# Decode attention with a mixer MLP on one core: five buffers of 32 KB per partition become three of 64 KB, and the softmax sums become running ones

## The chip, the cores and the metric

The kernel runs on one core of a Trainium2 chip. The metric is the device time of one execution in microseconds; the median of three runs before the change is 406.61 us (406.59 to 406.79). A core has a matrix engine (PE, with its weight loads shown as PEld), a vector engine (DVE), a scalar engine (ACT), GpSimd (POOL) and SyncE (SP), which here only issues transfers. Sixteen DMA engines carry the transfers of all queues. Data comes from HBM into SBUF (128 partitions); PE writes to PSUM.

## The reference

One token (`S = 1`, `D = 1024`) attends over a cache of 65,536 keys with 32 query heads in 4 groups of 8 that share a K and V, and the same token goes through a small mixer MLP. The result is their sum with the token.

```
xn = _layernorm(x)
# A: attention, Hq=32, Hkv=4, Sk=65536, Dh=128
q = (xn @ wq) per head
scores = einsum("bhqd,bhkd->bhqk", q, k) * (Dh ** -0.5)
p = softmax(scores)
a = einsum("bhqk,bhkd->bhqd", p, v) @ wo
# B: mixer MLP
h  = gelu(layernorm(xn) @ w1)
hs = (h, its four quarters shifted along the sequence) @ w2
x1 = xn + hs
b  = x1 + gelu(layernorm(x1) @ w3) @ w4
out = x + a + b
```

With a sequence of length 1 all four shifted quarters are zero. K and V are 16 MB each for a group (134 MB together), the weights some 36 MB; everything is bf16 and is read once: 169.88 MB.

## The kernel before

The cache of a group is cut into `NT = 4` blocks of `KEYS = 16384` keys; a block of K or V is 4 MB, 32 KB in each of the 128 partitions. All inputs but x pass through a pool `big` of `SLOTS = 5` buffers ("homes") of that size. `items` lists them in order: wq in two parts, then for each group K and V of the blocks 0 to 3 in turn and wo of the group, with w3 (two parts) after block 1 of group 0 and w1 after block 1 of group 1; at the end w2 and w4 in five pieces of 16, 8, 2, 1 and 1 rows of 1024 for each partition. `ensure` (L129) issues each load from SP (L118), four items ahead of the one that is computed; a load waits on SP until its home's last reader is done.

For a block of K (`compute_K`, L342) DVE transposes the home in place in four steps (L353), PE forms the scores from each quarter with the spread-out queries `qst` (L357, 32 matmuls into the PSUM tile `sc`), DVE takes the largest (L361), a short chain between PE and DVE spreads it over the partitions (L363 to L372), ACT takes the exponential (L374, with the row sum) and DVE transposes the result to `pT` (L377). `qst` has two buffers, filled for later groups by GpSimd (L257, L380).

For a block of V (`compute_V`, L382) PE sums `pT` against V into the one PSUM buffer `oacc` (L389, 32 matmuls). Each block has its own maximum. For blocks 0 to 2 ACT copies `oacc` to a tile `ob` (L394). After the last block `group_end` (L399) weighs the four partial results by the exponentials of their maxima (L404 to L414), folds them over the partitions with four matmuls against `selbig` (L417) and one against `sel8big` (L419) and makes `oT5`, with which `compute_wo` adds to the output row in `psB` (L160). w2 and w4 add to the same row; after the last piece of w4, ACT and DVE copy a half of it each and ACT and SP issue a store each (L336 to L340).

At the start x comes in two small loads on ACT's queue (L123, L125). The layernorms, masks and selectors are built from it while wq loads; gelu rows of w3 and w1 are turned round through DRAM on GpSimd's queue (`bounce`, L286).

The order of the instructions in an engine's queue is not the order of the text: the tile framework makes it when it builds the kernel, along with the waits.

Of the kernel before, what the change touches and what calls it, by code (L numbers as in the profile page):

```python
# [15 lines left out]
SLOTS = 5  # L16
KEYS = 16384
LOOKAHEAD = 4
# [4 lines left out]
def kernel(  # L23
# [36 lines left out]
    small = ctx.enter_context(tc.tile_pool(name="small", bufs=2))  # L60
    big = ctx.enter_context(tc.tile_pool(name="big", bufs=SLOTS))
    ppool = ctx.enter_context(tc.tile_pool(name="pp", bufs=2))
    obpool = ctx.enter_context(tc.tile_pool(name="obp", bufs=NT))
    scr_pool = ctx.enter_context(tc.tile_pool(name="scr", bufs=2))
    ogpool = ctx.enter_context(tc.tile_pool(name="ogp", bufs=1))
# [7 lines left out]
    wq_v = A_wq.rearrange("(p c) n -> p c n", c=DC)  # L73
    w3_v = B_w3.rearrange("(p c) f -> p c f", c=DC)
# [5 lines left out]
    w4_start = [sum(W4_PIECES[:i]) for i in range(len(W4_PIECES))]  # L80

    items = [("wq", 0), ("wq", 1)]
    for g in range(HKV):
        for r in range(NT):
            items += [("K", g, r), ("V", g, r)]
            if (g, r) == (0, 1):
                items += [("w3", 0), ("w3", 1)]
            if (g, r) == (1, 1):
                items += [("w1",)]
        items += [("wo", g)]  # L90
    items += [("w2",)] + [("w4", q) for q in range(len(W4_PIECES))]

    st = {}

    def slot():
        return big.tile([P, KEYS], BF16, name="slot")

    def issue(item):
        kind = item[0]
        t = slot()  # L100
        if kind == "wq":
            src = wq_v[:, 4 * item[1]:4 * item[1] + 4, :].rearrange("p c n -> p (c n)")
        elif kind == "w3":
            src = w3_v[:, 4 * item[1]:4 * item[1] + 4, :].rearrange("p c n -> p (c n)")
        elif kind == "w4":
            c0 = w4_start[item[1]]
            src = w4_v[:, c0:c0 + W4_PIECES[item[1]], :].rearrange("p c n -> p (c n)")
        elif kind == "w1":
            src = w1_v
        elif kind == "w2":  # L110
            src = w2_v
        elif kind == "wo":
            src = wo_v[item[1]]
        else:
            cache = A_k_cache if kind == "K" else A_v_cache
            _, g, r = item
            src = cache[0, g, r * KEYS:(r + 1) * KEYS, :].rearrange("(p k) d -> p (k d)", p=P)
        nc.sync.dma_start(out=t[:, 0:src.shape[-1]], in_=src)  # L118
        st[item] = t
# [4 lines left out]
    x_row_bf = const.tile([1, D], BF16, name="x_row_bf")  # L124
# [4 lines left out]
    def ensure(upto):  # L129
        while n_issued[0] <= min(upto, len(items) - 1):  # L130
            issue(items[n_issued[0]])
            n_issued[0] += 1
# [3 lines left out]
    ident_bf = const.tile([P, P], BF16, name="ident_bf")  # L136
    make_identity(nc, ident_bf[:])
# [4 lines left out]
    ones_f = const.tile([P, P], F32, name="ones_f")  # L142
    nc.gpsimd.memset(ones_f[:], 1.0)
    xpad = const.tile([P, DC, 32], BF16, name="xpad")
    nc.gpsimd.memset(xpad[:], 0.0)
    xpad2 = const.tile([P, DC, 32], BF16, name="xpad2")
    nc.gpsimd.memset(xpad2[:], 0.0)
    QW = 4 * 520
    qst = []
    for i in range(2):  # L150
        q_ = const.tile([P, QW], BF16, name=f"qst{i}")
        nc.gpsimd.memset(q_[:], 0.0)
        qst.append(q_)
# [11 lines left out]
    xT = const.tile([P, DC], F32, name="xT")  # L165
    nc.vector.tensor_copy(out=xT[:], in_=x_bf[:])

    def layernorm(src, tag):
        rowsum = const.tile([P, 1], F32, name=f"ln_rowsum_{tag}")
        nc.vector.reduce_sum(out=rowsum[:], in_=src[:], axis=AX.X)  # L170
        pm = ps_M.tile([P, 512], F32, name="pm_ln", tag="pm")
        nc.tensor.matmul(pm[:, 0:1], lhsT=ones_f[:], rhs=rowsum[:], start=True, stop=True)  # L172
        negmean = const.tile([P, 1], F32, name=f"ln_negmean_{tag}")
        nc.vector.tensor_scalar(out=negmean[:], in0=pm[:, 0:1], scalar1=-1.0 / D, scalar2=None, op0=ALU.mult)
        cen = const.tile([P, DC], F32, name=f"ln_cen_{tag}")
        nc.vector.tensor_scalar(out=cen[:], in0=src[:], scalar1=negmean[:, 0:1], scalar2=None, op0=ALU.add)
        sq = const.tile([P, DC], F32, name=f"ln_sq_{tag}")
        rowsq = const.tile([P, 1], F32, name=f"ln_rowsq_{tag}")
        nc.vector.tensor_tensor_reduce(out=sq[:], in0=cen[:], in1=cen[:], scale=1.0, scalar=0.0,
                                       op0=ALU.mult, op1=ALU.add, accum_out=rowsq[:])  # L180
        nc.tensor.matmul(pm[:, 1:2], lhsT=ones_f[:], rhs=rowsq[:], start=True, stop=True)
        std = const.tile([P, 1], F32, name=f"ln_std_{tag}")
        nc.scalar.activation(out=std[:], in_=pm[:, 1:2], func=ACTF.Sqrt, bias=eps_t[:, 0:1], scale=1.0 / D)
        rstd = const.tile([P, 1], F32, name=f"ln_rstd_{tag}")
        nc.vector.reciprocal(out=rstd[:], in_=std[:])
        normed = const.tile([P, DC], F32, name=f"ln_out_{tag}")
# [9 lines left out]
    ln_s1 = const.tile([P, 1], F32, name="ln_s1")  # L196
    nc.vector.tensor_scalar(out=ln_s1[:], in0=rstd1[:], scalar1=1.0, scalar2=None, op0=ALU.add)
    ln_s2 = const.tile([P, 1], F32, name="ln_s2")
    nc.vector.tensor_tensor(out=ln_s2[:], in0=negmean1[:], in1=rstd1[:], op=ALU.mult)
    accx = scr_pool.tile([1, NOUT], F32, name="accx", tag="scr")  # L200
    nc.vector.tensor_scalar(out=accx[:], in0=x_row_bf[:], scalar1=ln_s1[0:1, 0:1], scalar2=ln_s2[0:1, 0:1],
                            op0=ALU.mult, op1=ALU.add)
    for j in range(2):
        row_acc(j, ones_f[0:1, 0:1], accx[0:1, 512 * j:512 * (j + 1)])


    sel32 = const.tile([P, 32], F32, name="sel32")
# [9 lines left out]
    selbig = const.tile([P, 4, P], F32, name="selbig")  # L217
    for cg in range(4):
        nc.vector.tensor_copy(out=selbig[:, cg, :].rearrange("p (hl dd) -> p hl dd", dd=16),
                              in_=sel32[:, 8 * cg:8 * cg + 8].unsqueeze(2).to_broadcast([P, 8, 16]))  # L220
# [4 lines left out]
    psel = const.tile([P, 4, P], BF16, name="psel")  # L225
    iv = ident_bf[:].rearrange("p (b i r) -> p b r i", b=2, r=2)
# [25 lines left out]
    def fill_qst(g, eng):  # L252
        wv = qst[g % 2][:].rearrange("p (cg x) -> p cg x", x=520)[:, :, 0:512].rearrange(
            "p cg (bp c) -> p cg bp c", c=128)
        for a in range(4):
            sl = slice(32 * a, 32 * a + 32)
            eng.tensor_copy(out=wv[sl, :, :, 32 * a:32 * a + 8],  # L257
                            in_=qsel[sl, :, 8 * g:8 * g + 8].unsqueeze(1).to_broadcast([32, 4, 4, 8]))

    def compute_wq(part):  # L260
        wt = st.pop(("wq", part))[:].rearrange("p (c n) -> p c n", n=HQ * DH)
        acc = rows_product("psq", part, wt, xpad, 512, 8)
        if part == 1:
            qrow = scr_pool.tile([P, 2, 512], BF16, name="qrow", tag="scr")
            nc.vector.tensor_copy(out=qrow[:, 0, :], in_=acc[:, 0, :])
            nc.scalar.copy(out=qrow[:, 1, :], in_=acc[:, 1, :])
            del st["psq"]
            pt = ps_M.tile([P, 8, P], BF16, name="pm_qt", tag="pm")
            for bk in range(2):
                for c4 in range(4):  # L270
                    nc.tensor.transpose(pt[:, 4 * bk + c4, :], qrow[:, bk, 128 * c4:128 * c4 + 128], ident_bf[:])

            qT = const.tile([P, HQ], BF16, name="qT")
            for bk in range(2):
                nc.vector.tensor_copy(
                    out=qT[:, 16 * bk:16 * bk + 16].rearrange("p (j c) -> p j c", j=4),
                    in_=pt[:, 4 * bk:4 * bk + 4, :].rearrange("p c (j u) -> p j c u", j=4)[:, :, :, 0])
            pq = ps_M.tile([P, 4, HQ], F32, name="pm_qs", tag="pm")
            for bp in range(4):
                nc.tensor.matmul(pq[:, bp, :], lhsT=psel[:, bp, :], rhs=qT[:], start=(bp == 0), stop=(bp == 3),  # L280
                                 skip_group_check=True)
            nc.vector.tensor_copy(out=qsel[:], in_=pq[:])
            fill_qst(0, nc.vector)
            fill_qst(1, nc.gpsimd)
# [8 lines left out]
    def compute_w3(part):  # L293
        wt = st.pop(("w3", part))[:, 0:4 * F].rearrange("p (c n) -> p c n", n=F)
        acc = rows_product("psh", part, wt, xpad2, FW, 8)
        if part == 1:
            hrow = scr_pool.tile([P, 2, FW], BF16, name="hrow", tag="scr")
            nc.scalar.activation(out=hrow[:], in_=acc[:, :, 0:FW], func=ACTF.Gelu_apprx_tanh)
            del st["psh"]
            st["hT"] = bounce(hrow[:].rearrange("(j u) b n -> j u b n", u=32)[:, 0],  # L300
                              lambda f: f.rearrange("(b j n) -> j b n", b=2, j=4), FC, "h")

    def compute_w1():
        wt = st.pop(("w1",))[:, 0:DC * D].rearrange("p (c n) -> p c n", n=D)
        acc = rows_product("psh1", 0, wt, xpad2, 512, 2)
        h1row = scr_pool.tile([64, 512], BF16, name="h1row", tag="scr")
        nc.scalar.activation(out=h1row[:], in_=acc[0:64, 0, :], func=ACTF.Gelu_apprx_tanh)
        grow = scr_pool.tile([64, 512], BF16, name="grow", tag="scr")
        nc.vector.memset(grow[:], 0.0)
        cq = D // 4  # L310
        for grp, shift in enumerate((1, -1, 2, -2)):
# [161 lines left out]
```

## Time and profile before

| what | value |
|---|---|
| median of three runs | 406.61 us |
| the profiled execution, its own time | 406.69 us |
| its span, first to last instruction | 404.8 us |
| PE / DVE / ACT / POOL busy | 61% / 53% / 9% / 3% |
| read from HBM | 169.88 MB, 420 GB/s over the span |
| L353, transposes of K | x64, 142.3 us, 2281 ns each |
| L357, scores | x512, 131.6 us |
| L389, weighted sum of V | x512, 56.0 us |
| L374, exponential | x16, 17.8 us |
| L409, joining of partial results | x12, 0.75 us each |
| L394, copies of oacc | x12, 586 ns each |

The page divides the span into 40 slices of 10.1 us and gives each engine's busy share in tenths. Groups of instructions are listed by line, with the idle time of the engine before them and what ended it. DVE's longest waits are for K's loads (61.1 us before L353), PE's are for DVE (48.0 us before L389, for `pT`; 40.9 before L357, for the transposes). The granted clock of PE is 0.796 on the mean. The chain of work that ended last is 54% DMA, 23% PE and 17% DVE.

### The profile page before, as it was taken

To read this page: it belongs to the slowest core of one execution; us is meant where nothing else is said; L and a number is where in the kernel's file an instruction comes from. 1 tells how busy PE (TensorE), PEld (TensorE's weight loads), DVE (VectorE), ACT (ScalarE), POOL (GpSimd) and SP (SyncE) were. 2 spreads that over 40 slices of the span, in tenths; PEclk is the share of its full clock that TensorE was granted. 3 is DMA by queue.
4 is the path that set the end of the run, shared out by engine and by line. 5 is a ranking of instruction groups with operands and counts; after the bars stand their busy time and mean duration, and the time that the engine had idled before them with its cause. 6 is when DMAs were issued, how large, how long until landed. Compare 5 with 4: busy or idle time off the path is not lost.

```text
span 404.8 us, 3326 instructions
## 1 busy us (share of the span) xinstructions
PE 245.7 (61%) x1400; PEld 95.7 (24%) x1400; DVE 215.7 (53%) x235; ACT 37.7 (9%) x60; POOL 11.2 (3%) x30
## 2 busy tenths in 40 slices
PE   0385565328475847557657948384659474758456
PEld 0132222103132312112223313131233121213122
DVE  0419474017484848346665847475748383838500
ACT  0101101100201010120210010101010101010100
POOL 5001000000000000000010000000000000000000
PEclk9998878857795778768595868888958797679898
DMA  8999999999999999999999999999999999999993
GB/s 363 415 424 449 418 426 434 430 418 444 434 408 439 447 416 419 458 418 416 447 431 413 437 444 414 435 440 418 430 440 424 428 439 427 425 437 413 440 415 134
DMA packets 7065, 170.11 MB, mean 420 GB/s; under 512 B 1023, under 2 KB 1033, under 8 KB 1418
## 3 DMA queue, kind: packets, MB, share of 16 engines
q1 hardware_dynamic: 6772, 169.87, 98.0%
q8 instruction: 11, 0.18, 0.2%
q0 software_dynamic: 128, 0.02, 0.0%
q10 hardware_dynamic: 150, 0.01, 0.0%
q14 instruction: 4, 0.03, 0.0%
HBM read 169.88 MB, written 0.01 MB: 420 GB/s over the span
## 4 chain that ended last, share of the span: by engine, by line
DMA 54%; PE 23%; DVE 17%; ACT 2%; another core or an unknown queue 1%; issue 1%; DVEq 0%; ACTq 0%
DMA slot<-in_A_k_cache_dram 44%; DVE slot L353 11%; PE sc L357 10%; DMA slot<-in_B_w_dram 7%; PE psB L160 5%; PE oacc L389 4%; DMA x_bf<-in_A_x_dram 3%; DVE pT L377 2%; DVE mx L361 2%; ACT p_sb L374 2%; PE rows L244 1%; PE pm_e L417 1%; DVE m L365 0%; PE pm_mx L363 0%
## 5 line engine op out<-in xcount | busy, mean ns | idle before, releaser
L353 DVE STREAM_TRANSPOSE slot<-slot 128x2048 f32<-128x2048 f32 x64 | 142.3, 2281 | 61.1 <-DMA slot<-in_A_k_cache_dram 61.1
L357 PE MATMUL sc<-slot,qst 128*128 128x512 bf16 x512 | 131.6, 411 | 40.9 <-DVE slot L353 40.9
L389 PE MATMUL oacc<-slot,pT 128*32 128x512 bf16 x512 | 56.0, 616 | 48.0 <-DVE pT L377 48.0
L357 PEld LDWEIGHTS <-qst 128*128 128x128 bf16 x512 | 51.6, 103 | 125.1 <-issue 45.9
L361 DVE TENSOR_REDUCE mx<-sc 128x1 f32<-128x1024 f32 x16 | 19.6, 1225 | 34.7 <-PE sc L357 34.7
L374 ACT ACTIVATE p_sb<-sc,nball 128x1024 bf16<-128x1024 f32 x16 | 17.8, 1114 | 209.8 <-DVE nball L372 209.8
L389 PEld LDWEIGHTS <-pT 128*32 128x32 bf16 x512 | 17.5, 139 | 75.0 <-DVE pT L377 49.4
L377 DVE STREAM_TRANSPOSE pT<-p_sb 128x1024 bf16<-128x1024 bf16 x16 | 19.9, 1245 | 23.3 <-ACT p_sb L374 23.3
L244 PE MATMUL rows<-slot,xpad 128*32 128x512 bf16 (+1 forms) x144 | 13.6, 509 | 6.1 <-DMA slot<-in_B_w_dram 6.1
L363 PE MATMUL pm_mx<-ident_f,mx 128*1 128x128 f32 x16 | 4.3, 270 | 21.1 <-DVE mx L361 21.1
L160 PE MATMUL psB<-slot,oT 128*1 128x512 bf16 x64 | 12.6, 564 | 4.3 <-DVE oT L428 4.3
L394 ACT COPY ob<-oacc 128x512 f32<-128x512 f32 x12 | 7.0, 586 | 58.6 <-PE oacc L389 58.6
L160 PE MATMUL psB<-slot,dst_h 128*1 128x512 bf16 x56 | 7.9, 444 | 3.2 <-DMA slot<-in_B_w_dram 3.2
L370 PE MATMUL pm_mx<-ident_f,rep 1*128 1x1 f32 x16 | 3.5, 222 | 9.9 <-DVE rep L367 9.9
L417 PE MATMUL pm_e<-og,selbig 128*128 128x128 f32 x32 | 7.4, 403 | 3.4 <-DVE og L409 3.4
L244 PEld LDWEIGHTS <-xpad 128*32 128x32 bf16 x144 | 5.7, 127 | 15.0 <-issue 13.7
L172 PE MATMUL pm_ln<-ln_rowsum_a,ones_f 128*128 128x1 f32 x2 | 0.6, 348 | 13.6 <-DVE psel L229 13.6
L337 DVE CAST out<-psB 64x256 bf16<-64x256 f32 x1 | 0.4, 417 | 15.2 <-ACT out L336 15.2
L363 PEld LDWEIGHTS pm_mx<-ident_f,mx 128*1 128x1 f32 x16 | 1.3, 79 | 29.0 <-DVE mx L361 29.0
L417 PEld LDWEIGHTS pm_e<-og,selbig 128*128 128x128 f32 x32 | 6.3, 293 | 6.7 <-DVE og L409 6.7
L365 DVE TENSOR_REDUCE m<-pm_mx 1x8 f32<-1x128 f32 x16 | 4.4, 278 | 5.8 <-PE pm_mx L363 5.8
L374 ACT ACT_TABLE_LOAD x3 | 3.8, 1283 | 35.6 <-DVE nball L372 35.6
(97 smaller groups left out, 79.3 us busy)
## 6 DMA issues: line engine op xcount, KB each, us to landing
slot<-in_A_k_cache_dram SPq DMA_DIRECT2D x16, 4096.0 KB, 34.5
slot<-in_A_v_cache_dram SPq DMA_DIRECT2D x16, 4096.0 KB, 35.5
slot<-in_A_wq_dram SPq DMA_DIRECT2D x2, 4096.0 KB, 21.4
slot<-in_A_wo_dram SPq DMA_DIRECT2D x4, 2048.0 KB, 38.4
slot<-in_B_w_dram SPq DMA_DIRECT2D x2, 3584.0 KB, 42.6
slot<-in_B_w_dram SPq DMA_DIRECT2D x3, 2048.0 KB, 26.9
slot<-in_B_w_dram SPq DMA_DIRECT2D x1, 4096.0 KB, 27.8
slot<-in_B_w_dram SPq DMA_DIRECT2D x1, 512.0 KB, 16.1
```

The source lines that it names most:

```text
L160: nc.tensor.matmul(psB[32 * j:32 * j + 1, :], lhsT=lhsT, rhs=rhs, start=(not row_started[j]), stop=False, tile_position=(0, 32 * j), skip_ ...
L244: nc.tensor.matmul(acc[32 * j:32 * j + 32, bk, 0:width], lhsT=xp[:, c, :], rhs=wt[:, cl, ch * width:(ch + 1) * width], start=(c == 0), sto ...
L353: nc.vector.transpose(out=kf[:, cg, :], in_=kf[:, cg, :])
L357: nc.tensor.matmul(sc[:, hf, :], lhsT=qst[g % 2][:, o:o + 128], rhs=kr[:, cg, hf, :, bp // 2, :, bp % 2], start=(cg == 0 and bp == 0), sto ...
L361: nc.vector.reduce_max(out=mx[:], in_=sc[:].rearrange("p h n -> p (h n)"), axis=AX.X)
L363: nc.tensor.transpose(pm[0:1, 0:P], mx[:, 0:1], ident_f[:])
L365: nc.vector.reduce_max(out=m8[:], in_=pm[0:1, 0:P].rearrange("o (j h) -> o h j", h=8), axis=AX.X)
L374: nc.scalar.activation(out=p_sb[:], in_=sc[:], func=ACTF.Exp, bias=nball[:, r:r + 1], scale=SCALE, accum_out=lall[:, r:r + 1])
L377: nc.vector.transpose(out=pT[:], in_=p_sb[:])
L389: nc.tensor.matmul(oacc[32 * u:32 * (u + 1), :], lhsT=pT[:, hf, 32 * t:32 * (t + 1)], rhs=vt[:, :, hf, t, :], start=(hf == 0 and t < 4), s ...
L394: nc.scalar.copy(out=ob[:], in_=oacc[:])
L417: nc.tensor.matmul(pe[:, 0:P], lhsT=selbig[:, cg, :], rhs=og[:, 128 * cg:128 * (cg + 1)], start=(cg == 0), stop=(cg == 3))
```

## The change

The homes become three of 64 KB per partition, two loads ahead instead of four. K and V come in loads of 8 MB, two blocks (halves) in one, except the last K and the last V of group 3, which are loaded as two of 4 MB into one home. wq and w3 come whole. wo of groups 0 to 2 and w1 share one home after group 2; wo of group 3, w2 and the first piece of w4 share another; the other four pieces of w4 the last. The two halves of K are computed one after the other, then the two halves of V.

The four partial results of a group are no longer kept: a running minimum `nm` of the negated maxima, a factor `alpha` for what was summed so far, a running sum `ls` and a running result `og` replace `ob`, `nball`, `lall` and the weighing at the group's end. `og` is begun by an ACT copy and continued by DVE reading `oacc`. `selbig` is replaced by a mask `mask4` on `og` and `sel8big`. `qst` becomes one buffer, filled by DVE at the first block of each group. Many small tiles move into shared buffers (`early`, `one`, `tpool`), and the output is copied by ACT alone and stored in one transfer.

```diff
-SLOTS = 5
+SLOTS = 3
+SLOT = 32768
 KEYS = 16384
-LOOKAHEAD = 4
+HALVES = 2
+LOOKAHEAD = 2
...
-    ppool = ctx.enter_context(tc.tile_pool(name="pp", bufs=2))
-    obpool = ctx.enter_context(tc.tile_pool(name="obp", bufs=NT))
...
+    ppool = ctx.enter_context(tc.tile_pool(name="pp", bufs=1))
+    tpool = ctx.enter_context(tc.tile_pool(name="tp", bufs=2))
...
+    slots = [[("wq",)]]
     for g in range(HKV):
...
+        for t in range(BIG):
+            parts = range(HALVES) if (g, t) == (HKV - 1, BIG - 1) else (None,)
+            for kind in ("K", "V"):
+                slots.append([(kind, g, t, h) for h in parts])
+            if (g, t) == (0, 0):
+                slots.append([("w3",)])
+        if g == HKV - 2:
+            slots.append([("wo", i) for i in range(HKV - 1)] + [("w1",)])
+    n4 = len(W4_PIECES)
+    slots.append([("wo", HKV - 1), ("w2",), ("w4", 0)])
+    slots.append([("w4", q) for q in range(1, n4)])
...
+    def issue(pieces):
+        t = big.tile([P, SLOT], BF16, name="slot")
+        at = 0
+        for piece in pieces:
+            src = source(piece)
+            w = src.shape[-1]
+            nc.sync.dma_start(out=t[:, at:at + w], in_=src)
+            loaded[piece] = t[:, at:at + w]
...
-            nc.scalar.copy(out=o0[:], in_=psB[0:64, 0:256])
-            nc.vector.tensor_copy(out=o1[:], in_=psB[0:64, 256:512])
...
+            nc.scalar.copy(out=o0[:], in_=psB[0:64, :])
+            nc.scalar.dma_start(out=out[0, 0, :].rearrange("(j n) -> j n", j=2),
+                                in_=o0[:].rearrange("(j u) n -> j u n", u=32)[:, 0])
...
     def compute_K(g, r):
...
         if r == 0:
...
+            fill_qst(g, nc.vector)
...
+        nm = small.tile([P, 1], F32, name="nm")
+        old = st.get("nm")
+        if r == 0:
+            nc.vector.tensor_copy(out=nm[:], in_=pm[:, P:P + 1])
+        else:
+            nc.vector.tensor_tensor(out=nm[:], in0=pm[:, P:P + 1], in1=old[:], op=ALU.min)
+        p_sb = ppool.tile([P, 2, 512], BF16, name="p_sb", tag="p")
+        lb = small.tile([P, 1], F32, name="lb")
+        nc.scalar.activation(out=p_sb[:], in_=sc[:], func=ACTF.Exp, bias=nm[:, 0:1], scale=SCALE, accum_out=lb[:, 0:1])
+        if r > 0:
+            alpha = small.tile([P, 1], F32, name="alpha")
+            nc.scalar.activation(out=alpha[:], in_=old[:], func=ACTF.Exp, bias=nm[:, 0:1], scale=-1.0)
+            ls = small.tile([P, 1], F32, name="ls")
+            nc.vector.scalar_tensor_tensor(out=ls[:], in0=st["l"][:], scalar=alpha[:, 0:1], in1=lb[:],
+                                           op0=ALU.mult, op1=ALU.add)
...
-        if r < NT - 1:
-            ob = obpool.tile([P, 512], F32, name="ob")
-            nc.scalar.copy(out=ob[:], in_=oacc[:])
...
+        if r == 0:
+            st["og"] = one.tile([P, 512], F32, name="og", tag="og")
+            nc.scalar.copy(out=st["og"][:], in_=oacc[:])
+            return
+        alpha = st.pop(("alpha", g, r))
+        nc.vector.scalar_tensor_tensor(out=st["og"][:], in0=st["og"][:], scalar=alpha[:, 0:1], in1=oacc[:],
+                                       op0=ALU.mult, op1=ALU.add)
+        if r == NT - 1:
+            group_end(g, st.pop("og"))
...
+    def group_end(g, og):
+        lp = st.pop(("l", g))
+        nc.vector.tensor_tensor(out=og[:].rearrange("p (c d) -> p c d", c=4),
+                                in0=og[:].rearrange("p (c d) -> p c d", c=4),
+                                in1=mask4[:].unsqueeze(2).to_broadcast([P, 4, P]), op=ALU.mult)
...
+        nc.tensor.matmul(pe[:, P:P + 1], lhsT=sel8big[:], rhs=lp[:, 0:1], start=True, stop=True)
         for cg in range(4):
-            nc.tensor.matmul(pe[:, 0:P], lhsT=selbig[:, cg, :], rhs=og[:, 128 * cg:128 * (cg + 1)],
-                             start=(cg == 0), stop=(cg == 3))
...
+            nc.tensor.matmul(pe[:, 0:P], lhsT=sel8big[:], rhs=og[:, 128 * cg:128 * (cg + 1)],
+                             start=(cg == 0), stop=(cg == 3), skip_group_check=True)
...
-    for i, it in enumerate(items):
+    for i, pieces in enumerate(slots):
         ensure(i + LOOKAHEAD)
-        compute[it[0]](*it[1:])
+        for it in pieces:
+            if it[0] in ("K", "V"):
+                for h in range(HALVES):
+                    if it[3] in (None, h):
+                        compute[it[0]](it[1], HALVES * it[2] + h)
+            else:
+                compute[it[0]](*it[1:])
```

## The prediction, made before the changed kernel was run

> **What bounds the kernel now.** I read the page's slices and queue counts first, then the end of the chain of waits, then the timeline of one key block and of the start.
>
> ```profile
> span 404.8 us, 3326 instructions
> ...
> DMA  8999999999999999999999999999999999999993
> DMA packets 7065, 170.11 MB, mean 420 GB/s; under 512 B 1023, under 2 KB 1033, under 8 KB 1418
> ...
> q1 hardware_dynamic: 6772, 169.87, 98.0%
> ...
> slot<-in_A_k_cache_dram SPq DMA_DIRECT2D x16, 4096.0 KB, 34.5
> ```
>
> The 16 DMA engines are busy in every slice but the first and the last, and the packets of SP's queue alone fill 98.0% of 404.8 = 396.7 us. PE (61%) and DVE (53%) are far from full. A 4 MB load lands a median 34.5 us after its issue although it needs only 9.7 us of transfer (below): more than two others are queued ahead of it, so no load waits for its issue.
>
> ```profile
> 365.42 27.79 DMA slot<-in_B_w_dram
> 393.21 0.04 issue
> 393.26 7.49 PE psB L160 x54
> 400.76 0.40 PE psB L160 x2
> 401.18 0.38 ACT out L336
> 401.57 0.42 DVE out L337
> ```
>
> This is the end of the chain of waits (start, duration, what). The last weights land piece by piece and PE follows each: the end is the end of the stream plus a short tail. So the kernel is bound by its transfers from 1.8 us to about 400.3 us, and a change can gain only in three places: the price of a byte, a pause in the stream, the tail. It loses if it opens a pause, or if the arithmetic ends after the stream.
>
> **Larger loads.** The bytes stay at 169.87 MB. The loads become 31 instead of 47. Packets can be counted: 47 x 128 rows + 47 x 16 completion packets + 4 for the output = 6772, the page's number, so today one row of up to 32 KB is one packet. The trace's packet records give a median of 1216 ns for 32 KB, 614 for 16 KB, 161 for 4 KB, 85 for 2 KB. So a packet has a fixed part of 2 x 614 - 1216 = 12 ns, or 2 x 85 - 161 = 9 ns at the small end. wq and the K and V loads that are merged are 3840 packets of 32 KB, 240 on each engine (the last K and V and w4's first piece keep theirs). If a row of 64 KB goes as one packet, 120 fixed parts vanish, and 8 more with w3's merged rows: 128 x 9 to 12 ns, 1.2 to 1.5 us. 16 completion packets less, at 9 ns, add 0.1. No packet above 32 KB is in the trace, so this has a lower end too: 28 KB packets (1062 ns) are 2 ns cheaper per 32 KB than the 32 KB ones, and if that went on, 240 x 2 ns would be a loss of 0.5 us. I take -1.2 us: the gain, since two of three steps in size show a fixed part, at its low price.
>
> Is the seam between two loads worth something? 32 KB in 1216 ns on 16 engines is 431 GB/s, 9.73 us for 4 MB, and the 98.0% leaves no room for seams: 0. The Trainium skill, "DMA: Bandwidth & Descriptors", section "Anatomy of one DMA — SWDGE (gpsimd) path", puts about 2 us of fixed time on every DMA; if it were exposed, 16 fewer loads would save an estimated 32 us, but its own text lays it on completion, which here lies under the next load's packets, and the 98.0% agrees.
>
> Rows now lie 64 KB apart in memory instead of 32 KB. wq's two loads already step 64 KB from row to row, and their packets have a median of 1213 ns against 1216: 0. The same page's section "Latency and other measured facts" speaks against the change: large power-of-two row pitches slow a copy, from 207 instead of 214 GB/s at 512 KiB downwards; taken over to 64 KB this would be 3%, an estimated 12 us, which wq's packets deny.
>
> **Three homes.** When K has landed at time T, its two halves need at most 16.0 us each (below), the last matmul that reads the home comes at T + 16.0 + 10.9 = T + 26.9, and the home is next filled two loads on, from T + 38.9: 12 us to spare. V is done by about T + 41 at the latest and its home is needed at T + 58.4: 17 us. At the start wq's home is needed at about 60 us and free by 39. SP's queue carries only loads behind such a wait; they lose nothing.
>
> **The start.** x_bf has eight 16 B packets per engine, each between two packets of SP: 12.3 us to land. With 64 KB packets it is 8 x 1.2 = 9.7 us later, 22.7 us. The q chain ends at 32.9 now (first transpose), then 42.6; the first 8 MB of K land at 1.8 + 16.78 MB / 431 = 40.7 or up to 2 us later on the slowest engine. So it costs 0 to 2 us of compute, taken up in the 17 us that w3's transfer gives. Without that cover, the 12 us of the homes stand before the stream.
>
> **Compute for one block**, from the timeline:
>
> ```profile
> 344.61 8.89 DVE L353 STREAM_TRANSPOSE slot<-slot 128x2048 f32<-128x2048 f32 x4 [4.76 <-DMA slot<-in_A_k_cache_dram]
> ...
> 356.54 1.23 DVE L361 TENSOR_REDUCE mx<-sc 128x1 f32<-128x1024 f32 x1 [3.04 <-PE sc L357]
> ...
> 360.47 1.25 DVE L377 STREAM_TRANSPOSE pT<-p_sb 128x1024 bf16<-128x1024 bf16 x1 [1.33 <-ACT p_sb L374]
> 361.77 3.60 PE L389 MATMUL oacc<-slot,pT 128*32 128x512 bf16 x32 [2.83 <-DVE pT L377]
> ...
> 192.10 1.28 ACT L374 ACT_TABLE_LOAD   x1 [16.02 <-DVE nball L372]
> ```
>
> A K block is a chain of 16.0 us on DVE (279.94 to 296.00 in the chain of waits): 12.0 busy (8.89 + 1.23 + 1.25 + three small ones of 0.65) and 4.0 of waiting for PE and ACT. Then V takes 3.6 us on PE, today under the next block's transposes, because ACT copies the result off. After the change DVE reads it (0.75 us, the price of L409), and a transpose queued behind that waits for V. Alpha on ACT and the sum on DVE add at most 0.3 us a block; fill_qst on DVE 1.08 a group, early; the mask an estimated 0.65 (near the 0.75); og's first copy stays on ACT.
>
> But two blocks now land together. Does DVE wait its 4.0 us, or take the second block's transposes meanwhile? The build orders a queue by readiness, not by the text:
>
> ```profile
> 13.27 0.16 DVE L170 TENSOR_REDUCE ln_rowsum_a<-xT 128x1 f32<-128x8 f32 x1
> 13.35 0.22 DVE L229 COPY psel<-ident_bf 128x128 bf16<-128x128 bf16 x1
> 13.48 0.18 DVE L208 TENSOR_TENSOR sel<-ident_f 128x32 f32<-128x32 f32 x1
> ...
> 14.17 0.16 DVE L174 TENSOR_SCALAR ln_negmean_a<-pm_ln 128x1 f32<-128x1 f32 x1 [0.37 <-PE pm_ln L172]
> ```
>
> L229 and L208 come after L174 in the text but before it in DVE's queue, filling its wait for PE. So I expect the second half's transposes in the first half's waits: a pair takes 32.0 - 4.0 = 28.0 us, with V and its reading (4.4) 32.4, with a group's end (8.4, below) 36.4, under the 38.9 us in which the two loads of a pair arrive. Nothing piles up.
>
> **The end of group 3** is the only place where compute could outlast the stream. Behind the K pair of blocks 0 and 1 follow 36.7 MB, 85 us at 431 GB/s, so it lands at 315. Add 1.3 for the table load (w1's gelu now stands just before; 192.10 shows it in the chain), 28.0, V and its reading 4.4: 348.7, when K of block 2 is there. Blocks 2 and 3 come as two loads: 32.0 in turn, 28.0 if filled. Then V 3.6, reading 0.75, mask 0.65, the four pe matmuls 2.1 (L417 in the middle groups), oT5 1.3: 385.1 to 389.1. From there wo 3.6, w2 1.9, w4 56 x 0.118 (16 in 1.89) = 6.6 if nothing is late: 397.2 to 401.2 for PE's end, against 401.2 now and, with the stream 1.3 us shorter, 399.9 (the 315 moves up by 1.1 with it, so 400.1 at the latest). Cost 0 to 0.2.
>
> **The tail.** Today PE ends at 401.16, then copies on ACT (0.38) and DVE (0.42) one after the other, and SP's issue ends at 402.65. Now one ACT copy of 512 columns (0.59, as L394) and one issue (0.61): 402.36. Gain 0.2 to 0.3.
>
> **Sum:** profiled run 406.69 us (its span 404.8 and 1.9 around it; the median of the runs is 406.61) - 1.2 (packets) - 0.1 (fewer completion packets) - 0.2 (tail) + 0.1 (end of compute) = 405.3 us. Own range 404.4 to 406.0.
>
> **Rivals.** *(a) Rows still move in 32 KB packets.* For: nothing above 32 KB is seen. Against: 28 KB and 32 KB rows were each taken whole. Then only completion packets and tail remain: 406.69 - 0.3 = 406.4, no change.
>
> *(b) The softmax chain outlasts the stream.* If DVE's queue keeps to the text, each pair costs 32.0, and group 3 runs 315 + 1.3 + 32.0 + 4.4 + 32.0 + 8.4 = 393.1; with 12.1 for wo, w2 and w4 PE ends at 405.2, less 1.1 for the earlier stream: 404.1 against 401.2 today, so 406.69 + 2.9 - 0.2 = 409.4. If PE runs wo and pe at the faster pace of today's last group (1.89 for 3.58, 1.16 for 2.08), it is 2.6 less, 406.8; I price it at 408.5. It decides once oT5 of group 3 is done after 389.0 (401.16 - 12.1); today that is 386.4. For it: a DVE instruction reading V's result now stands in the queue; against: the fill shown at 13.35.
>
> *(c) The stream pauses or slows:* a home freed over 12 us late, or 64 KB packets dearer than two of 32 KB. Today's loads and wq's packets speak against both. Each us of pause is a us of time; at 1% dearer packets 4 us, some 410.
>
> **Chances.** Forecast 0.50, (a) 0.20, (b) 0.20, (c) 0.10. Changes under 0.2% (405.8 to 407.4) count as none, about what a measurement of this kernel can tell. Forecast: 0.42 faster, 0.08 same. (a): 0.03, 0.15, 0.02 slower. (b): 0.01 same, 0.19 slower. (c): 0.01 and 0.09. Sums: 0.45, 0.25, 0.30. The range of 404.3 to 408.6 leaves out the upper half of (b) and most of (c).
>
> **What would show it.** Right: SP's queue with 31 x 16 completion packets and 4464 packets in all (31 x 128 rows); x_bf landing near 22; SP's waits long before the stream needs a home; L353 of a second half between the first half's mx and pT; oT5 of group 3 before 389. Wrong: SP's packets near 6500 (a); DVE idle before each pT and oT5 after 389 (b); a slice with the DMA below 9 in mid-stream, or fewer than 431 GB/s (c).

## The result and the profile after

The changed kernel takes **405.18 us** (median of 10 runs, 404.77 to 405.98), the kernel before, in runs beside it, 406.52 us (406.36 to 406.79). The ratio is 0.9969 with a 95% interval of 0.996 to 0.9979: a gain of 1.34 us, 0.3%. The forecast was 405.3 us. The profiled execution took 405.86 us; it is one of the longer ones, and why they differ by up to a microsecond is part of what follows.

The page of the changed kernel, its span, slices and SP's queue (q1: packets, MB, share of the 16 engines' span):

```profile
span 404.1 us, 3274 instructions
...
DMA  9999999999999999999999999999999999999992
DMA packets 4756, 170.10 MB, mean 421 GB/s; under 512 B 765, under 2 KB 773, under 8 KB 1158
...
q1 hardware_dynamic: 4464, 169.87, 97.7%
```

SP's queue has 4464 packets, 31 x 128 rows and 31 x 16 completion packets: a row of 64 KB is one packet. No slice in mid-stream is below 9. 97.7% of 404.1 us is 394.8 us of packets, where 98.0% of 404.8 us were 396.7. In the trace's packet records the median for 64 KB is 2419 ns; two of 32 KB took 2 x 1216 = 2432. The last byte lands at 398.54 us instead of 400.27, 1.73 us earlier.

DVE's timeline of the first pair of K halves (start, duration, what; in brackets the idle time before it and what ended it):

```profile
22.77 0.17 DVE L186 CAST early<-x_bf 128x8 f32<-128x8 bf16 x1 [21.36 <-DMA x_bf<-in_A_x_dram]
...
41.93 13.28 DVE L359 STREAM_TRANSPOSE slot<-slot 128x2048 f32<-128x2048 f32 x6 [0.80 <-DMA slot<-in_A_k_cache_dram]
55.13 1.19 DVE L367 TENSOR_REDUCE mx<-sc 128x1 f32<-128x1024 f32 x1
56.24 2.29 DVE L359 STREAM_TRANSPOSE slot<-slot 128x2048 f32<-128x2048 f32 x1
58.46 0.24 DVE L371 TENSOR_REDUCE m<-pm_mx 1x8 f32<-1x128 f32 x1
58.62 2.29 DVE L359 STREAM_TRANSPOSE slot<-slot 128x2048 f32<-128x2048 f32 x1
```

Six transposes run in a row, two of them already of the second half, and its last two stand between the first half's `mx`, `m` and what follows: the queue is filled by readiness. In these lines DVE waits for nothing once K has landed; in the rest of the pair, which ends at 69.0 us, it waits four times, 3.6 us in all. The small load `x_bf` comes at 22 us, and the first transpose waits for K (0.80 us), not for the q chain.

The end, in the timeline of all engines:

```profile
379.13 0.23 DVE L441 TENSOR_SCALAR oT<-o,rl 128x8 bf16<-128x8 f32 x1
...
379.42 1.89 PE L180 MATMUL psB<-slot,oT 128*1 128x512 bf16 x16 [1.06 <-DVE oT L441]
...
381.73 1.89 PE L180 MATMUL psB<-slot,dst_g 128*1 128x512 bf16 x16 [0.42 <-DMA slot<-in_B_w_dram]
...
391.44 9.07 PE L180 MATMUL psB<-slot,dst_h 128*1 128x512 bf16 x56 [7.83 <-DMA slot<-in_B_w_dram]
...
400.56 0.58 ACT L346 CAST out<-psB 64x512 bf16<-64x512 f32 x1 [28.75 <-PE psB L180]
401.17 0.61 ACTq L347 DMA_DIRECT2D out_dram<-out  x1
```

`oT5` of the last group (named `oT` here) is done at 379.4 us, 7 us earlier than before. PE then has nothing to do for 7.83 us, and its 56 matmuls of w4 take 9.07 us, where the kernel before needed 7.88 after an idle time of 3.19:

```profile
393.26 7.88 PE L160 MATMUL psB<-slot,dst_h 128*1 128x512 bf16 x56 [3.19 <-DMA slot<-in_B_w_dram]
```

So PE ends at 400.5, 2.0 us after the last byte; before it was 0.9. Of the 1.73 us that the stream gained, 1.1 are lost again there in this execution. PE's weight loads in the same stretch, one for each matmul, show how:

```profile
391.45 0.09 PEld L180 LDWEIGHTS <-dst_h 128*1 128x1 bf16 x3 [8.12 <-issue]
391.83 0.13 PEld L180 LDWEIGHTS <-dst_h 128*1 128x1 bf16 x2 [0.29 <-issue]
...
396.95 0.13 PEld L180 LDWEIGHTS <-dst_h 128*1 128x1 bf16 x2 [0.29 <-issue]
397.33 2.68 PEld L180 LDWEIGHTS <-dst_h 128*1 128x1 bf16 x26 [0.25 <-issue]
```

Until 397.3 us two loads start every 0.43 us (391.83, 392.25 and so on); then 26 run in 2.68 us, 0.10 each. For its first 5.9 us after the idle time PE goes at half its pace.

### The profile page after: what moved, and what is told of

It reads as the page before. It is cut to its first block, busy times and chain, and to the rows that moved or that the text cites. A ratio compares the mean times of both kernels' runs of the same rounds, so it can differ in the third digit from the quotient of the medians.

```text
span 404.1 us, 3274 instructions
## 1 busy us (share of the span) xinstructions
PE 229.9 (57%) x1400; PEld 92.7 (23%) x1400; DVE 214.1 (53%) x244; ACT 34.7 (9%) x60; POOL 5.9 (1%) x17
## 3 DMA queue, kind: packets, MB, share of 16 engines
q1 hardware_dynamic: 4464, 169.87, 97.7%
## 4 chain that ended last, share of the span: by engine, by line
DMA 63%; DVE 27%; PE 8%; ACT 1%; issue 0%; SPq 0%; ACTq 0%; DVEq 0%
DMA slot<-in_A_k_cache_dram 51%; DVE slot L359 22%; DMA slot<-in_B_w_dram 12%; PE oacc L410 3%; DVE mx L367 2%; PE psB L180 2%; PE sc L363 2%; DVE pT L400 1%; ACT p_sb L386 1%; DVE m L371 0%; PE pm_mx L376 0%; SPq L128 0%; DVE qst L276 0%; DVE og L418 0%; DVE rep L373 0%
## 5 line engine op out<-in xcount | busy, mean ns | idle before, releaser
L363 PE MATMUL sc<-slot,qst 128*128 128x512 bf16 x512 | 137.6, 424 | 91.5 <-DVE slot L359 91.4
L410 PE MATMUL oacc<-slot,pT 128*32 128x512 bf16 x512 | 43.9, 500 | 3.8 <-ACT og L415 2.1
L386 ACT ACTIVATE p_sb<-sc,nm 128x1024 bf16<-128x1024 f32 x16 | 17.8, 1113 | 177.0 <-DVE nm L383 112.9
L418 DVE SCALAR_TENSOR_TENSOR og<-og,alpha,oacc 128x512 f32<-128x512 f32 x12 | 8.9, 746 | 25.1 <-PE oacc L410 25.0
L410 PEld LDWEIGHTS <-pT 128*32 128x32 bf16 x512 | 16.2, 116 | 23.2 <-issue 15.3
L263 PE MATMUL rows<-slot,xpad 128*32 128x448 bf16 (+1 forms) x80 | 7.1, 466 | 7.2 <-DMA slot<-in_B_w_dram 7.2
L180 PE MATMUL psB<-slot,oT 128*1 128x512 bf16 x64 | 8.2, 399 | 1.1 <-DVE oT L441 1.1
L431 PE MATMUL pm_e<-og,sel8big 128*128 128x128 f32 x32 | 4.6, 288 | 5.0 <-DVE og L425 5.0
L376 PEld LDWEIGHTS pm_mx<-ident_f,rep 1*128 1x128 f32 x16 | 2.3, 142 | 17.6 <-DVE rep L373 16.7
L180 PEld LDWEIGHTS <-dst_h 128*1 128x1 bf16 x56 | 3.0, 104 | 13.9 <-issue 12.2
```

The source lines that it names most:

```text
L180: nc.tensor.matmul(psB[32 * j:32 * j + 1, :], lhsT=lhsT, rhs=rhs, start=(not row_started[j]), stop=False, tile_position=(0, 32 * j), skip_ ...
L263: nc.tensor.matmul(acc[32 * j:32 * j + 32, bk, 0:width], lhsT=xp[:, c, :], rhs=wt[:, cl, ch * width:(ch + 1) * width], start=(c == 0), sto ...
L363: nc.tensor.matmul(sc[:, hf, :], lhsT=qst[:, o:o + 128], rhs=kr[:, cg, hf, :, bp // 2, :, bp % 2], start=(cg == 0 and bp == 0), stop=(cg = ...
L376: nc.tensor.transpose(pm[:, P:P + 1], rep[0:1, :], ident_f[0:1, 0:1])
L386: nc.scalar.activation(out=p_sb[:], in_=sc[:], func=ACTF.Exp, bias=nm[:, 0:1], scale=SCALE, accum_out=lb[:, 0:1])
L410: nc.tensor.matmul(oacc[32 * u:32 * (u + 1), :], lhsT=pT[:, hf, 32 * t:32 * (t + 1)], rhs=vt[:, :, hf, t, :], start=(hf == 0 and t < 4), s ...
```

## The experiments

Five questions: is it the number of loads or the length of a row that pays; what does the rest of the change do alone; does DVE's order decide; what do the homes give; and what costs the microsecond at the end. Unless said otherwise an edit is to the changed kernel, and the time is the median with the lowest and highest run, beside the kernel before in the same session (medians 406.52 to 406.59).

**1. All K and V homes filled by two loads of 4 MB** (45 loads; a half's rows are 32 KB)

```diff
-            parts = range(HALVES) if (g, t) == (HKV - 1, BIG - 1) else (None,)
+            parts = range(HALVES)
```

> The changed kernel, but every K and V home of 8 MB is filled by two loads of 4 MB, so rows are 32 KB again and 14 loads are added. Packet theory (the gain is the fixed part of a packet, 13 ns by the changed kernel's 64 KB packets of 2419 ns against twice 1216): 112 packets more on each engine cost 1.5 us, 14 completion packets 0.1, so the stream ends 1.6 us later and the time is 406.4 (406.1 to 407.0), near the kernel before; SP's queue shows 4464 + 14 x 144 = 6480 packets. Rival, the gain comes from the tail and the end of compute: 405.2, no change from the changed kernel. Rival, every seam between two loads costs about 2 us: some 430.

**2. The 31 loads kept, but each K and V row fetched as two rows of 32 KB that lie 4 MB apart**

```diff
-            nc.sync.dma_start(out=t[:, at:at + w], in_=src)
+            if piece[0] in ("K", "V") and piece[3] is None:
+                ...
+                nc.sync.dma_start(out=t[:].rearrange("p (h x) -> p h x", h=HALVES),
+                                  in_=rows.rearrange("(h p k) d -> p h (k d)", h=HALVES, p=P))
```

> The changed kernel with its 31 loads, but a K or V load of 8 MB takes two rows of 32 KB for each partition from two places 4 MB apart (the keys of a pair are dealt to partitions as in the kernel before). Load count and packet size come apart. Packet theory: 112 packets more on each engine, 1.5 us, 406.2 (405.9 to 406.9), with 4464 + 14 x 128 = 6256 packets in SP's queue. Rival, the number of loads is what pays: 405.2 as in the changed kernel.

Measured: 406.23 us (405.48 to 407.01, 11 runs; ratio 0.9989, 0.998 to 0.9998) for the first, 406.42 us (405.84 to 407.33, 11 runs; 0.9997, 0.9988 to 1.0006) for the second. SP's queue on their pages, first the 45 loads, then the 31:

```profile
q1 hardware_dynamic: 6480, 169.87, 97.9%
```

```profile
q1 hardware_dynamic: 6256, 169.87, 98.0%
```

Summed from the packet records, a DMA engine is busy 396.11 and 396.17 us on the mean, against 394.61 in the changed kernel; the last byte lands at 399.45 and 399.60, against 398.54. Fourteen loads more or less make no difference that the runs can tell; the length of the rows, and with it the number of packets, does. The two runs also part the row pitch from the packet: rows lie 64 KB apart in the first and 32 KB in the second, and a packet of 32 KB has a median of 1215 and 1218 ns. The gain of the larger loads is that of longer rows, not of fewer seams.

**3. The tail of before: two copies, two stores**

```diff
-            o0 = tpool.tile([64, 512], BF16, name="out0", tag="pT")
-            nc.scalar.copy(out=o0[:], in_=psB[0:64, :])
...
+            nc.scalar.copy(out=o0[:], in_=psB[0:64, 0:256])
+            nc.vector.tensor_copy(out=o1[:], in_=psB[0:64, 256:512])
```

> The changed kernel with the tail of before: the row is copied in halves by ACT and DVE and stored by two transfers from ACT and SP. Theory: ACT 0.38 and DVE 0.42 in turn and SP's issue 0.63 against one copy of 0.58 and one issue of 0.61: 0.2 to 0.3 us slower, 405.4 (405.0 to 405.8). Rival, the tail is the main part of the gain: 406.2 or more. Rival, the tail is hidden: 405.2.

Measured: 405.30 us (405.04 to 405.87, 9 runs; 0.9971, 0.9961 to 0.998). The medians differ by 0.12, less than the runs scatter. The four lowest runs are 405.04 to 405.17, the five lowest of the changed kernel 404.77 to 404.86: by these about 0.27. The traces agree: from the start of ACT's copy to the end of the last issue it is 1.45 us here (400.46 to 401.91), 1.22 in the changed kernel (400.56 to 401.78). The tail is worth 0.1 to 0.3 us.

**4. The first piece of w4 cut in two, so that PE may begin earlier**

```diff
-W4_PIECES = (16, 8, 2, 1, 1)
+W4_PIECES = (8, 8, 8, 2, 1, 1)
...
-    slots.append([("wo", HKV - 1), ("w2",), ("w4", 0)])
-    slots.append([("w4", q) for q in range(1, n4)])
+    slots.append([("wo", HKV - 1), ("w2",), ("w4", 0), ("w4", 1)])
+    slots.append([("w4", q) for q in range(2, n4)])
```

> The changed kernel with w4's first piece of 4 MB split into two of 2 MB (8, 8, 8, 2, 1, 1). In the changed kernel's profile PE stands idle for 7.8 us before the piece of 4 MB lands at 391.4 and then needs 9.1 us for 56 matmuls, at first 0.21 us each, ending 2.0 us after the last landing, where before it was 0.9. Theory (the two levels of the runs, 404.8 and 405.8, are PE's pace at the end): with half the piece done 4.9 us earlier PE ends 0.9 us after the last landing in every run: 404.8 with no run above 405.2. Rival (the levels are the stream's): still two levels, median 405.2. One load and one completion packet more cost nothing visible.

Measured: 406.35 us (404.66 to 407.26, 11 runs; 0.999, 0.9978 to 1.0002). The expectation failed: 1.2 us slower than the changed kernel. PE's timeline, from the longest of the eleven runs (407.26):

```profile
386.78 1.89 PE L180 MATMUL psB<-slot,dst_h 128*1 128x512 bf16 x16 [2.96 <-DMA slot<-in_B_w_dram]
391.67 3.05 PE L180 MATMUL psB<-slot,dst_h 128*1 128x512 bf16 x16 [3.00 <-DMA slot<-in_B_w_dram]
396.61 5.28 PE L180 MATMUL psB<-slot,dst_h 128*1 128x512 bf16 x24 [1.89 <-DMA slot<-in_B_w_dram]
```

The early piece gets 16 matmuls out of the way, but PE now waits about 3 us twice. The first 16 go at 0.118 us each, the last 24 at 0.22, and these end 3.2 us behind the last byte (398.67): PE ends at 401.9, where the changed kernel ended at 400.5. The half pace lies now where nothing covers it. Two of the 11 runs (404.66 and 404.68) are as short as the changed kernel's shortest, so the loss does not come in every run.

**5. DVE's queue kept to the text's order** (the second half's transposes stand behind the first half's `pT`)

```diff
+            if st.get("last_pT") is None:
                 nc.vector.transpose(out=kf[:, cg, :], in_=kf[:, cg, :])
+            else:
+                with tc.issue_after(st["last_pT"]):
+                    nc.vector.transpose(out=kf[:, cg, :], in_=kf[:, cg, :])
...
-        nc.vector.transpose(out=pT[:], in_=p_sb[:])
+        st["last_pT"] = nc.vector.transpose(out=pT[:], in_=p_sb[:]).ins
```

> The changed kernel, with DVE's queue kept to the text: the transposes of a second half are queued behind the first half's last transpose (pT). This is rival (b) made true. Theory (the fill is what keeps the softmax chain inside the stream): a pair takes 32 us and not 28, oT5 of group 3 comes at 387 to 391 and not at 379, and PE ends 0 to 5 us after 400.5: 405.2 to 410, most likely 407. The stream shows no pause, since a home is still free 12 us early. Rival, there is so much room that the order is no matter: 405.2 with oT5 under 387.

Measured: 410.30 us (408.38 to 411.09, 5 runs; 1.0099, 1.0083 to 1.0114), slower than before and than the most likely 407 of the expectation. DVE's timeline from the K pair of group 3's blocks 0 and 1:

```profile
312.89 8.89 DVE L363 STREAM_TRANSPOSE slot<-slot 128x2048 f32<-128x2048 f32 x4 [13.41 <-DMA slot<-in_A_k_cache_dram]
325.09 1.22 DVE L371 TENSOR_REDUCE mx<-sc 128x1 f32<-128x1024 f32 x1 [3.31 <-PE sc L367]
...
330.28 1.25 DVE L404 STREAM_TRANSPOSE pT<-p_sb 128x1024 bf16<-128x1024 bf16 x1 [2.61 <-ACT p_sb L390]
331.45 8.85 DVE L363 STREAM_TRANSPOSE slot<-slot 128x2048 f32<-128x2048 f32 x4
...
393.09 0.23 DVE L445 TENSOR_SCALAR oT<-o,rl 128x8 bf16<-128x8 f32 x1
```

Here the brackets are back: 3.31 us before `mx`, 2.61 before `pT`, and only then the second half's four transposes. `oT5` is done at 393.3 instead of 379.4. The last byte still lands at 398.51, in the slices the stream is as full as ever, and yet the kernel is slower: the arithmetic has become the bound. The trace is of the run of 408.38 us, the lowest of the five: PE ends at 403.0 us there instead of 400.5, which is the 2.5 us between it and the changed kernel's profiled run of 405.86. The other four runs, 410.05 to 411.09, left no trace; their granted clock is lower (0.791 to 0.802, against 0.810), and whether that is the cause is not shown.

**6. Two homes instead of three, one load ahead**

```diff
-SLOTS = 3
+SLOTS = 2
...
-LOOKAHEAD = 2
+LOOKAHEAD = 1
```

> The changed kernel with two homes and one load ahead. Theory (a home is free 21 us after K has landed, with 19.5 us of V's transfer to cover it, and its next load needs some 2 us more to start): the stream pauses about 3.5 us for every pair and a little at the weights, 8 to 10 pauses, 432 to 442, and the slices show the DMA below full through the whole span. Rival, the spare time of the homes was misjudged and a third home is not needed: 405 to 408.

Measured: 438.38 us (a single run), as expected. From its page:

```profile
span 436.6 us, 3273 instructions
...
DMA  9999979999959896999789879986999967999993
...
q1 hardware_dynamic: 4464, 169.87, 91.3%
```

The same packets, but holes in the stream: with only one load ahead a home is not free in time. Three homes are enough, two are not.

**7. The kernel before with the running sums alone** (with `mask4` in place of `selbig`; five homes, 4 MB loads, text otherwise as before)

```diff
-        nc.vector.tensor_copy(out=nball[:, r:r + 1], in_=pm[:, P:P + 1])
...
+        if r == 0:
+            nc.vector.tensor_copy(out=nm[:], in_=pm[:, P:P + 1])
+        else:
+            nc.vector.tensor_tensor(out=nm[:], in0=pm[:, P:P + 1], in1=old[:], op=ALU.min)
...
+        nc.vector.scalar_tensor_tensor(out=st["og"][:], in0=st["og"][:], scalar=alpha[:, 0:1], in1=oacc[:],
+                                       op0=ALU.mult, op1=ALU.add)
```

> The kernel before with only the softmax part of the change: running minimum, alpha, running sum and og, mask4 in place of selbig; five homes of 32 KB and all loads as before. Theory (with one block to a load there is nothing to fill DVE's waits, and the reading of V's result stands before the next transposes): blocks 1 and 2 of a group take 16.0 + 3.6 + 0.8 = 20.4 us against 19.5 of transfer, so group 2 and 3 gather some 5 us, oT5 of group 3 comes near 391 and not at 386.4, and PE ends 0 to 2.5 us late: 406.4 to 408.9, most likely 407.5. Rival, running sums cost nothing by themselves: 406.5. Rival, they bring part of the gain: under 406.0.

Measured: 406.27 us (406.05 to 406.32, 11 runs; 0.999, 0.9982 to 0.9999). This too failed the expectation, on the good side: no loss but 0.3 us of gain. DVE's waits (what waited for what: us in all, times, longest):

```profile
DVE og L406 <- PE oacc L398: 42.0, 12, 3.6
DVE mx L354 <- PE sc L350: 36.1, 16, 3.2
DVE slot L346 <- DMA slot<-in_A_k_cache_dram: 27.1, 6, 15.9
```

The price that was feared is there: DVE stands 42.0 us in front of V's results. But it is paid out of the waits for K's loads, which were 61.1 us before and are 27.1 now. `oT5` comes at 388.1, 1.7 us later than before and still in time. The gain itself sits in the stream: the last byte lands at 399.85 instead of 400.27, with the same 6772 packets, and PE ends 0.87 us after it in both. Half of that 0.42 is in the packets (a DMA engine is busy 396.45 us on the mean instead of 396.67). Why, no run here tells; it stays open.

**8 and 9. PE kept at work before w4's first piece**: 32, then 8 matmuls on data that is already on the chip, into an accumulator that nothing reads, put behind w2's last matmul (the trace has records of 31 and 7 of them)

```diff
+FILLER = 32
...
+        with tc.issue_after(st["w2_last"]):
+            idle = ps_S.tile([P, 2, 512], F32, name="idle", tag="sc")
+            for i in range(FILLER):
+                nc.tensor.matmul(idle[:, 0, :], lhsT=qst[:, 0:128], rhs=qst[:, 0:512], start=True, stop=True)
```

> The changed kernel with 32 extra matmuls on PE behind w2 (qst against qst into an unused PSUM tile, never read), to fill the 7.8 us in which PE waits for w4's first piece. Theory (PE's pace at the end depends on how long it has stood still before): fillers end near 391, w4's first 32 matmuls run at 0.12 us each and not 0.21, PE ends under 1 us after the last landing of about 398.5 in every run: 404.3 to 404.8, one level. Rival (the two levels of the runs are the stream's, or the granted clock's by its mean): still two levels, median 405.2. Rival (more PE work late costs time): 405.5 or more.

> The same with 8 extra matmuls, which end near 386, 5 us before w4's first piece lands. Theory (the standing still just before counts, not the amount of work): as the changed kernel, 405.0 to 405.9 with runs at two levels. Rival (any added work helps, or a mere shift of the queue): 404.3 to 404.8 as with 32.

Measured: 404.84 us with 32 (404.62 to 405.15, 5 runs; 0.9958, 0.9945 to 0.997), 405.28 us with 8 (404.66 to 406.24, 10 runs; 0.997, 0.996 to 0.9979). Eight of them end at 386.7, and PE waits again:

```profile
391.51 8.60 PE L181 MATMUL psB<-slot,dst_h 128*1 128x512 bf16 x56 [4.78 <-DMA slot<-in_B_w_dram]
```

Eight fillers change nothing that the runs can tell; enough of them to reach w4's first piece take the long runs away: with 32, none of the five is above 405.15.

**10 to 12. The changed kernel again, the 32 fillers again, and the fillers with the split rows of experiment 2, on one chip**

> The changed kernel once more, beside the next two on the same chip: 405.2, runs from 404.8 to 406.0.

> The changed kernel with 32 filler matmuls before w4 once more, for a comparison with the changed kernel on one chip. Theory (it takes away the upper level of the runs): median 404.8, all runs within 404.6 to 405.2, 0.3 to 0.5 below the changed kernel. Rival (the first look was a draw of mostly quick runs): the same spread and median as the changed kernel.

> Rows of K and V in two pieces of 32 KB, with the filler, so that PE's pace at the end no longer blurs the price of the packets. Packet theory: the last landing moves by 1.0 to 1.5 us against the filler kernel, so 405.8 to 406.3 in a narrow spread. Rival (the difference of 1.2 us seen without the filler was PE's pace): 404.8.

| kernel | median, us | runs | ratio to before (95%) | PE's end in the profiled run |
|---|---|---|---|---|
| changed | 405.21 | 404.76 to 406.19 (9) | 0.9971 (0.9961 to 0.998) | 399.62 |
| with 32 fillers | 404.68 | 404.67 to 405.07 (5) | 0.9958 (0.9946 to 0.9971) | 399.35 |
| split rows, 32 fillers | 405.85 | 405.61 to 407.24 (11) | 0.9986 (0.9977 to 0.9995) | 400.65 |

The profiled run of the changed kernel is one of 404.96 us this time, where the first was one of 405.86. PE's timeline and its weight loads:

```profile
391.67 7.95 PE L180 MATMUL psB<-slot,dst_h 128*1 128x512 bf16 x56 [3.55 <-DMA slot<-in_B_w_dram]
```

```profile
391.67 1.16 PEld L180 LDWEIGHTS <-dst_h 128*1 128x1 bf16 x13 [3.85 <-issue]
393.13 0.14 PEld L180 LDWEIGHTS <-dst_h 128*1 128x1 bf16 x2 [0.29 <-issue]
...
396.11 2.94 PEld L180 LDWEIGHTS <-dst_h 128*1 128x1 bf16 x27 [0.29 <-issue]
```

`oT5` is done at 383.1 us here and not at 379.4, PE waits 3.55 us, begins at the full pace, and goes at half of it only from about 393 to 396. It ends 0.87 us after the last byte (398.75), as in the kernel before. So the 0.90 us between the two profiled runs of the same kernel are PE's end, 400.51 against 399.62, and not the stream.

PE's timeline with the fillers:

```profile
383.83 7.08 PE L342 MATMUL idle<-qst 128*128 128x512 bf16 x31
391.53 3.62 PE L181 MATMUL psB<-slot,dst_h 128*1 128x512 bf16 x32 [0.62 <-DMA slot<-in_B_w_dram]
396.44 2.91 PE L181 MATMUL psB<-slot,dst_h 128*1 128x512 bf16 x24 [1.29 <-DMA slot<-in_B_w_dram]
```

The 56 matmuls take 3.62 + 2.91 = 6.53 us instead of 9.07 or 7.95, with a wait for the stream in between: PE follows each piece again, and ends 0.85 us after the last byte (398.50). The windows view says the same with the granted clock (columns: us, then the busy time of PE, PEld, DVE, ACT and POOL with the number of instructions, the clock, the DMA share, GB/s), first the two profiled runs of the changed kernel (405.86 and 404.96), then that with the fillers:

```profile
391.00:399.00 8.00, 7.55 (x44) 2.49 (x45) 0.00 (x0) 0.00 (x0) 0.00 (x0) 0.61 0.68 272
```

```profile
391.00:399.00 8.00, 7.33 (x54) 2.70 (x54) 0.00 (x0) 0.00 (x0) 0.00 (x0) 0.79 0.70 283
```

```profile
391.00:399.00 8.00, 6.18 (x56) 2.40 (x55) 0.00 (x0) 0.00 (x0) 0.00 (x0) 1.00 0.68 277
```

With PE's pace out of the way the rows can be priced cleanly: 405.85 - 404.68 = 1.17 us for 1792 packets more (14 loads x 128), and the last byte (399.79 against 398.50) 1.29 us later. One run of the split rows, 407.24, stands alone above ten that lie within 0.4 us; its cause was not found. The median with 32 fillers is 0.34 us under the changed kernel's by the first runs of each and 0.53 side by side, and none of its ten runs is above 405.15, where 10 of the changed kernel's 19 are.

## Why the prediction was right, and what it missed

The forecast of 405.3 us is 0.1 above the median, for the reason it gave. That it is so close is in part luck: two sizes that it did not have, one for and one against, nearly cancel in it.

- **Packets, -1.2 us**: right. 4464 packets, as counted beforehand, and 1.17 us by the split rows with fillers (K and V alone; the 256 merged rows of wq and w3 were not tried). A 64 KB row is taken whole, which ended rival (a).
- **Seams and row pitch, 0**: right. The 45 loads and the 31 with 32 KB rows have the same stream (396.11 and 396.17 us), the first with rows 64 KB apart; the 64 KB row costs 13 ns less than two rows, not more. The 2 us that the forecast cites for a transfer stand, as the section's heading says, for transfers that GpSimd issues, and these loads are SP's: the runs show no such price for them.
- **Tail, -0.2 us**: right within what the runs can tell, 0.1 to 0.3.
- **Homes**: right. The next load into the first K's home was issued 21.2 us after K had landed (41.93 to 63.15 us), where 26.9 were worked out and 38.9 allowed; the run with two homes shows what stands behind that margin, 33 us.
- **Start**: right. `x_bf` at 22.7 was forecast, 22.77 measured; the first transpose at 42.6, measured 41.93, because the q chain was done by 41.1 and K was the last to come.
- **Rival (b)** did not occur, but its working was tested by putting DVE in the text's order. `oT5` was worked out for 393.1 (392.0 with the 1.1 us of the earlier stream) and came at 393.3 in the profiled run. That this is so close is luck: the last K pair began at 312.9 and not at 315, and from there to `oT5` it took 80.4 us and not 78.1. For the time the rival had 406.8 to 409.4, booked at 408.5; the profiled run took 408.38, the median 410.30. So what made the change harmless is the order of DVE's queue; the price of losing it is 5 us in the medians, of which a trace shows 2.5.
- **End of group 3, 385.1 to 389.1**: too late by 6 to 10 us in the first profiled run, by 2 to 6 in that of experiment 10 (383.1). In the first, the terms were set too high: the K pair took 27.1 us with the table load (312.79 to 339.86), 1.3 + 28.0 forecast; blocks 2 and 3 were filled into each other's waits, V of block 2 lay under block 3, and the last V took 1.91 us on PE and not 3.6 (3.56 in experiment 10).
- **The step that failed**: "w4 56 x 0.118 (16 in 1.89) = 6.6 if nothing is late". It took PE's pace from w2, which runs right behind wo, and put it behind a wait. The profile of the kernel before already had 7.88 us there. The early end of group 3 made that wait 7.83 us, the matmuls took 9.07, and the loss, forecast as +0.1 for the end of compute, is +0.53 us in the medians (405.21 against 404.68; 405.18 against 404.84 by the first runs of each), 1.1 in the first profiled run and nothing in the second. The mechanism is one that the forecast did not have: arithmetic that ends too early can cost time.
- **Against it** stand about 0.3 us that came with the running sums, in the stream, cause unknown. They were measured on the kernel before; whether they carry over to the changed one no run shows by itself, but the last byte fits: 1.29 us for the rows and 0.42 for the sums against 1.73 measured. Together, in the medians: -1.17 - 0.2 + 0.53 - 0.32 = -1.2, of 1.34 measured. The rest is within the scatter of the medians.

## What to carry to other kernels

In a kernel bound by its transfers, count packets before loads: here a contiguous row of 64 KB goes as one packet and 1792 fewer packets were worth 1.2 us of 405, while 14 fewer loads were worth nothing. Before transfers are made larger, ask in which order each engine's queue will meet the work that now arrives at once, since the same loads with another order were 5 us slower. And look at what the last consumer of the stream does while it waits: a PE that stood idle before the last pieces went at half its pace for 3 to 6 us when they came, and 32 idle matmuls helped where smaller pieces did harm.

## What the runs showed of the hardware

- **PE after an idle time.** Behind 0.62 us of waiting it went on at 0.11 us a matmul (granted clock 1.00 in that stretch). Behind 3.19 us (the kernel before), 4.78 (8 fillers), 6.38 (45 loads) and 7.83 us (changed) it took 0.21 us a matmul from the first on. Behind 3.00 us (experiment 4) and 3.55 us (experiment 10) it began at the full pace and fell to half of it about 0.5 and 1.3 us later. The 56 matmuls took 7.88, 8.60, 9.08 and 9.07 us in the first four, but 7.87 in the run with split rows after 7.82 us: the half pace lasted 3.4 us there (392.63 to 396.00), 3.2 in the kernel before (393.26 to 396.48) and 5.9 in the changed kernel. So the wait brings it about, and does not fix how long it lasts. This goes with the scatter of the changed kernel's runs: two groups among the first ten (404.77 to 404.86 and 405.5 to 405.98), no gap among the nine of experiment 10 (404.76 to 406.19). The Trainium skill, "TensorE: Matmul & The Clock Gate", section "Part 1: The HAM clock gate", says that the clock is halved after an idle window of about 3.4 us, restored after as much busy time, and that the window runs free of the kernel; the late falls, the 3.2 to 5.9 us and their spread agree with that by and large, though waits of 3.00 and 3.19 us were enough in two kernels here.
- **A small load beside large packets.** `x_bf` landed 12.3 us after its issue beside 32 KB packets and 22.0 beside 64 KB: the difference is 9.7 us, which is 8 times the 1.2 us that a packet became longer, for eight small packets per engine that each wait for a large one. The packet records show the steps: the starts of the small packets lie 1.22 us apart before and 2.42 us after, one large packet each.
